# A spectral mixing kernel: the last transform stage runs two units behind the mixing, and the shrinking becomes one ScalarE Relu and one VectorE pass

## The chip, the cores and the metric

The kernel runs on one core of a Trainium2 chip. Its time is the device time of one execution in microseconds (us). TensorE (PE) multiplies matrices, VectorE (DVE), ScalarE (ACT) and GpSimd (POOL) work elementwise, and SyncE (SP) only issues transfers. Each engine works through its own queue in order and waits on semaphores for the others. Matmul results land in PSUM, which has eight banks; everything else sits in SBUF or in device memory.

## What is computed

For each of 8 batches of 3072 x 256 values, the reference takes a real Fourier transform along the sequence, mixes the 256 channels with a complex matrix, adds a bias, shrinks both parts towards zero by 0.01 and transforms back. A feed-forward network with two weight matrices and a piecewise square gate follows.

```python
X = np.fft.rfft(x, axis=1)
Yr = Xr @ w_r - Xi @ w_i + b_r
Yi = Xr @ w_i + Xi @ w_r + b_i
Yr = np.sign(Yr) * np.maximum(np.abs(Yr) - lam, 0.0)
Yi = np.sign(Yi) * np.maximum(np.abs(Yi) - lam, 0.0)
y = np.fft.irfft(Yr + 1j * Yi, n=3072, axis=1)
h = y @ w_in
g = np.where(h >= 1, h, np.where(h <= -1, 0.0, (h + 1) ** 2 / 4))
out = g @ w_out
```

## The kernel before

The transform is cut into factors of 48 and 64. Stage 1 is the 48-point factor over half batches of rows, stage 2 the 64-point factor, then the channels are mixed, then stages 3 and 4 undo the two factors. Products are made with operands split into a rounded part (hi) and a rest (lo), three matmuls to a product.

**The mixing loop** (`for u in range(UN + 3)`, `UN` = 96) handles one unit per iteration: two of the 24 frequency groups of a batch, so 12 units (`NU`) to a batch. The order in which instructions are recorded is the order in which each engine's queue holds them; nothing rearranges them. In iteration u the kernel records:

- `split_X_hi` (L258): two ScalarE copies of stage 2's result of unit u-1 out of PSUM, `Xd` (the imaginary half) and `Xh` (the rounded whole);
- `difference` (L267): VectorE makes the difference `Xd` of the two halves. For the first unit of a batch it also makes a few two-column tiles (`Xe`, `e0`);
- `mix_shared` (L307): six matmuls of unit u-2 into the bank `ps_mix`; `take_shared` (L313): VectorE adds the bias to the result and keeps it as `shift`;
- `split_X_lo` (L283) and `split_difference` (L288): the rests `Xl`, `Xdl` on VectorE and the rounded `Xdh` on ScalarE;
- `stage3` (L342) of unit u-3: matmuls that read `y` of that unit, and a ScalarE copy `ust` of the result, which `store_u` writes to `u_d` one iteration later;
- `stage1` in the iterations that have one (two of three after the first batch, none in the last ones), with two ScalarE copies;
- `mix_rest` (L319): twelve matmuls of unit u-2 on top of the same bank, six more for a batch's first unit; `add_bias` (L327): VectorE adds `shift` and writes `y`;
- `shrink` (L332): VectorE clamps `y` to +-0.01 (`yc`, L335) and subtracts that from `y` (L336);
- `stage2` (L241) of unit u.

So `stage3` of unit u-3 in iteration u needs the `shrink` that was recorded at the end of iteration u-1. Between the two, TensorE has `stage2` of unit u-1 and `mix_shared` of unit u-2.

Three calls `weights()` in an iteration convert the network's double precision weights a step at a time, two units to a weight (32 weights, so some 64 units from u = 2 on); the steps run on VectorE (`man`, `scl`), ScalarE (`parts`, `winh`, `wout`) and GpSimd (`both`, `wpair`, `winl`). `half4` runs stage 4 on an eighth of the first batch; eight of them are spread over the last iterations. The network follows the loop and runs on from there.

`ust` and `ps_mix` have two buffers, `y` (tag `ya`) two, `yc` (tag `yb`) one, and stage 3's bank (tag `E`) one.

Of the kernel before, what the change touches and what calls it, by code (L numbers as in the profile page):

```python
# [10 lines left out]
F32 = mybir.dt.float32  # L11
# [5 lines left out]
P = 128  # L17
# [86 lines left out]
def tile_fft_mix_moe(  # L104
# [44 lines left out]
    z_first = keep.tile([P, G, D], F32, tag="wout", name="z_first")  # L149
    c2_sb = keep.tile([P, R1], F32, name="c2_sb")  # L150
    half = keep.tile([P, 1], F32, name="half")

    c1_sb = first_st.tile([P, 2, HP], F32, name="c1_sb")
    t_sb = mixing.tile([P, G, P], F32, name="t_sb")
# [76 lines left out]
                nc.sync.dma_start(zh[b][k, :, j : j + HT, :], z[e * HP : e * HP + R1])  # L231


    zin, xp, dp, yp, ust = {}, {}, {}, {}, {}

    def load_z(u):
        b, v = divmod(u, NU)
# [20 lines left out]
    def split_X_hi(u):  # L258
        ps = xp[u]
        _, im = both(ps)  # L260
        dp[u] = mixing.tile([P, ND, P], F32, tag="Xd", name="Xd")
        nc.scalar.copy(dp[u], im)
        hi = mixing.tile([P, ND, 2, 2, R2], F32R, tag="Xh", bufs=2, name="Xh")
        nc.scalar.copy(hi, ps)
        xp[u] = ps, hi

    def difference(u):  # L267
        ps, _ = xp[u]
        re, _ = both(ps)
        dif = dp[u]  # L270
        at = slice(0, 1)
        if u % NU == 0:
            e = mixing.tile([P, ND, 1], F32, tag="Xe", name="Xe")
            nc.vector.scalar_tensor_tensor(
                out=e, in0=re[:, :, at], scalar=-1.0, in1=dif[:, :, at], op0=ALU.mult, op1=ALU.subtract
            )
            split(nc.vector, e0[0][:, :, at], e0[1][:, :, at], e)
        nc.vector.tensor_tensor(out=dif, in0=re, in1=dif, op=ALU.subtract)
        if u % NU == 0:
            nc.vector.tensor_copy(dif[:, :, at], re[:, :, at])  # L280

    def split_X_lo(u):
        ps, hi = xp[u]  # L283
        lo = mixing.tile([P, ND, 2, 2, R2], F32R, tag="Xl", bufs=2, name="Xl")
        nc.vector.tensor_tensor(out=lo, in0=ps, in1=hi.bitcast(F32), op=ALU.subtract)
        xp[u] = hi, lo

    def split_difference(u):  # L288
        dif = dp[u]
        hi, lo = dp[u] = [mixing.tile([P, ND, P], F32R, tag=f"Xd{k}", bufs=2, name=f"Xd{k}") for k in "hl"]  # L290
        nc.scalar.copy(hi, dif)
        nc.vector.tensor_tensor(out=lo, in0=dif, in1=hi.bitcast(F32), op=ALU.subtract)

    def mixed(out, pairs, start):
        n = 0
# [13 lines left out]
    def mix_shared(u):  # L309
        ps = yp[u] = pools["ps"].tile([P, 2, D], F32, tag="C", bufs=2, name="ps_mix")  # L310
        mixed(ps[:, 0, :], [(dp.pop(u), "i")], True)
# [15 lines left out]
    def add_bias(u):  # L327
        y = fold.tile([P, 2, D], F32, tag="ya", bufs=2, name="y")
        nc.vector.tensor_tensor(out=y, in0=yp[u], in1=shift, op=ALU.add)  # L329
        yp[u] = y  # L330

    def shrink(u):  # L332
        y = yp[u]
        c = fold.tile([P, 2, D], F32, tag="yb", name="yc")
        nc.vector.tensor_scalar(out=c, in0=y, scalar1=-LAM, scalar2=LAM, op0=ALU.max, op1=ALU.min)  # L335
        nc.vector.tensor_tensor(out=y, in0=y, in1=c, op=ALU.subtract)  # L336

    def stage3(u):
        b, v = divmod(u, NU)
        y = yp.pop(u)  # L340
        ps = pools["ps"].tile([P, 2, 2, D], F32, tag="E", name="ps_i1")[:, :, 0, :]
        for c in range(2):  # L342
            for gi in range(2):
                rows = slice(gi * HP, (gi + 1) * HP)
                nc.tensor.matmul(  # L345
                    ps[:, gi, :],
                    lhsT=ti_sb[rows, v, c, :],
                    rhs=y[rows, c, :],
                    start=c == 0,
                    stop=c == 1,  # L350
                    tile_position=(gi * HP, 0),
                )
        ust[u] = fold.tile([P, 2, D], F32, tag="ust", bufs=2, name="ust")
        nc.scalar.copy(ust[u], ps)

    def store_u(u):
        b, v = divmod(u, NU)
        nc.sync.dma_start(ug[b][:, 2 * v : 2 * v + 2, :], ust.pop(u))
# [292 lines left out]
    with tc.manual_schedule():  # L651
# [3 lines left out]
        idle = win[0][NP - 1][:, 0:1, :]  # L655
        nc.vector.memset(idle.bitcast(F32), 0.0)
        nc.vector.memset(half, 0.5)
        for x in e0:
            nc.vector.memset(x.bitcast(F32), 0.0)
        wst = []  # L660
# [53 lines left out]
        def half4(tags="AB"):  # L714
            c = next(four)
            stage4(c, [bank(k, 2 if k == "D" else 1) for k in tags])
            stage4_out(c, [nc.scalar.copy] * 2)

        U4 = UN - 8

        U_IN = UN - NU + 2

        WU = 2
        for u in range(UN + 3):
            hs_u = halves(u)
            at = lambda lag: 0 <= u - lag < UN
            weights = more_weights if WU <= u < 85 else lambda: None
            while stored < hs_u.start:
                store_z(stored)
                stored += 1  # L730
            if at(4):
                store_u(u - 4)
            if u == NU:
                wout = keep.tile([P, NF, 2, D], F32R, tag="wout", name="wout")
            if u + 1 < NU:
                load_ti(u + 1)
            if 0 < u < NU - 2:
                load_t(2 * u + 4, 2 * u + 6)
            if u == WU - 1:
                load_weights(0)  # L740
                load_weights(1)
            if u == 10:
                nc.sync.dma_start(c2_sb, c2)
            if NU <= u + 2 < UN:
                load_z(u + 2)
            if at(1):
                split_X_hi(u - 1)
                difference(u - 1)
            if at(2):
                mix_shared(u - 2)  # L750
                take_shared(u - 2)
            if at(1):
                split_X_lo(u - 1)
                split_difference(u - 1)
            weights()
            if at(3):
                stage3(u - 3)
            for h in hs_u:
                stage1(h, "AB", [nc.scalar.copy] * 2)
                x_ahead(h)  # L760
            if U4 <= u < U4 + 4 or u == UN:
                half4()
            weights()
            if at(2):
                mix_rest(u - 2)
                add_bias(u - 2)
                weights()
                shrink(u - 2)
            if u < UN:
                stage2(u)  # L770
            if u == U_IN:
                for _ in ws:
                    pass
                first_st.release()
                pools["in"] = right("in")
                pools["ops0"] = right("ops0")
                for c in range(3):
                    load_u(c)
            if u == UN - 3:
                prep_sums(0)  # L780
            if u == UN - 2:
                prep_split_hi(0, 0)
                prep_split_lo(0, 0)
            if u == UN - 1:
                prep_split_hi(0, 1)
                prep_split_lo(0, 1)
            if u == UN + 1:
                half4("DD")
                half4("AB")
                prep_split_hi(0, 2)  # L790
                prep_split_lo(0, 2)
                half4("DD")
        store_u(UN - 1)
        mixing.release()
        pools["ops1"] = right("ops1")
# [111 lines left out]
```

## Time and profile before

| | us |
|---|---|
| median of 3 runs | 2720.39 (2718.38 to 2722.28) |
| the profiled execution, its own time | 2722.25 |
| span of its trace, first to last instruction | 2720.3 |
| PE busy | 2636.1 (97%) |
| DVE busy | 2055.2 (76%) |
| ACT busy | 1622.5 (60%) |
| POOL busy | 330.7 (12%) |
| stage 3's first and last matmul start | 42.6 and 594.9 |

The trace gives the span; the execution's own time is 2 us more, for what lies around it. The last row bounds the mixing loop; the rest of the span is the network.

### The profile page before, as it was taken

The page shows a single profiled execution, that of the slowest core. Times are in us where ns is not written, and L with a number is a line of the kernel's source. Part 1 is how long each engine was busy: PE and PEld are TensorE (multiplying, and loading weights), DVE is VectorE, ACT ScalarE, POOL GpSimd, SP SyncE. Part 2 cuts the span into 40 slices and gives each one's busy share as a digit, 9 for nine tenths or more (in the row PEclk, how much of TensorE's full clock was granted, in tenths as well). Part 3 has the DMA queues.
Part 4 walks back from the last instruction along what each step waited for, and adds up shares of the span by engine and source line. Part 5 has one row for each costly group of instructions (what it writes and reads, how often), then busy time and mean ns, then how long its engine had stood idle before and what let it go on. Part 6 is the DMA issues. An engine that isn't in the chain of part 4 may idle for free.

```text
span 2720.3 us, 54586 instructions
## 1 busy us (share of the span) xinstructions
PE 2636.1 (97%) x22600; PEld 2385.1 (88%) x22600; DVE 2055.2 (76%) x3075; ACT 1622.5 (60%) x2909; POOL 330.7 (12%) x325
## 2 busy tenths in 40 slices
PE   8888889989999999999999999999999999999998
PEld 6666777779999999999999999999999999999998
DVE  5778886668777777777777777777777777777776
ACT  4445554446666666666666666666666666666665
POOL 2333220001000101001010101010101101010100
PEclk8999999999999999999999999999999999999999
DMA  7666766530000000000101000000000000100000
GB/s 218 193 191 198 208 203 187 146 101 9 22 25 23 26 22 27 23 26 22 31 22 30 21 28 21 28 20 28 21 28 21 28 27 22 34 15 23 9 17 16
DMA packets 114951, 160.65 MB, mean 59 GB/s; under 512 B 13072, under 2 KB 87440, under 8 KB 114704
## 3 DMA queue, kind: packets, MB, share of 16 engines
q1 hardware_dynamic: 114424, 156.97, 19.9%
q8 instruction: 178, 2.92, 0.4%
q14 instruction: 69, 0.57, 0.1%
q10 hardware_dynamic: 280, 0.20, 0.0%
HBM read 84.76 MB, written 72.35 MB: 58 GB/s over the span
## 4 chain that ended last, share of the span: by engine, by line
PE 90%; DVE 7%; ACT 1%; issue 1%; DMA 0%; SPq 0%; ACTq 0%
PE ps_xv L548 20%; PE ps_yz L548 15%; PE accB L604 13%; PE accA L604 13%; PE accB L607 7%; PE accA L607 7%; PE ps_mix L299 5%; PE ps_i L345 3%; PE ps_i L472 3%; PE ps_f L213 2%; DVE y L336 2%; DVE y L329 2%; DVE yc L335 1%; PE ps_f L247 1%; DVE scl L398 1%
## 5 line engine op out<-in xcount | busy, mean ns | idle before, releaser
L556 ACT COPY snap<-ps_xv 128x256 f32<-128x256 f32 x1152 | 424.2, 368 | 764.1 <-PE ps_xv L548 764.1
L590 DVE TENSOR_TENSOR gl<-h,gh 128x1024 fp32r<-128x1024 f32 x385 | 470.6, 1222 | 270.3 <-ACT gh L586 270.3
L560 DVE CUSTOM_DVE_ANT_0 h<-ps_yz,snap 128x256 f32<-128x256 f32 (+1 forms) x768 | 428.2, 558 | 227.6 <-PE ps_yz L548 194.6
L604 PE MATMUL accA<-wout,gh 128*128 128x512 f32 x1536 | 570.7, 393 | 0.0
L604 PE MATMUL accB<-wout,gh 128*128 128x512 f32 x1536 | 562.0, 399 | 0.0
L581 DVE SCALAR_TENSOR_TENSOR h<-h,r 128x1024 f32<-128x1024 f32 x385 | 480.7, 1249 | 0.0
L577 ACT ACTIVATE r<-h,half 128x1024 f32<-128x1024 f32 x385 | 443.3, 1151 | 2.0 <-DMA u_d<-ust 2.0
L548 PE MATMUL ps_xv<-oph,winh 128*128 128x256 f32 x1536 | 436.5, 284 | 1.2 <-ACT snap L556 0.9
L548 PE MATMUL ps_xv<-opl,winh 128*128 128x256 f32 x1536 | 433.5, 282 | 0.0
L607 PE MATMUL accB<-wout,gl 128*128 128x256 f32 x1536 | 432.4, 282 | 0.0
L607 PE MATMUL accA<-wout,gl 128*128 128x256 f32 x1536 | 431.4, 281 | 0.8 <-DVE gl L590 0.7
L548 PE MATMUL ps_xv<-oph,winl 128*128 128x256 f32 x1536 | 430.0, 280 | 0.0
L586 ACT CAST gh<-h 128x1024 fp32r<-128x1024 f32 x385 | 404.4, 1050 | 4.2 <-DVE h L581 4.1
L503 POOL TENSOR_TENSOR tsum<-yt 128x256 f32<-128x256 f32 x96 | 106.7, 1131 | 1982.1 <-DVE opl L524 1103.0
L604 PEld LDWEIGHTS accB<-wout,gh 128*128 128x128 f32 x1536 | 289.7, 189 | 56.8
L548 PE MATMUL ps_yz<-oph,winl 128*128 128x256 f32 x1152 | 326.2, 283 | 0.0
L548 PE MATMUL ps_yz<-oph,winh 128*128 128x256 f32 x1152 | 323.5, 281 | 1.9 <-DVE h L560 1.8
L548 PE MATMUL ps_yz<-opl,winh 128*128 128x256 f32 x1152 | 324.5, 282 | 0.0
L604 PEld LDWEIGHTS accA<-wout,gh 128*128 128x128 f32 x1536 | 287.8, 187 | 35.2
L548 PEld LDWEIGHTS ps_xv<-oph,winh 128*128 128x128 f32 x1536 | 288.0, 188 | 32.4 <-ACT snap L556 2.0
L548 PEld LDWEIGHTS ps_xv<-oph,winl 128*128 128x128 f32 x1536 | 291.2, 190 | 0.0
L607 PEld LDWEIGHTS accA<-wout,gl 128*128 128x128 f32 x1536 | 288.8, 188 | 1.8 <-DVE gl L590 1.8
(106 smaller groups left out, 4282.3 us busy)
## 6 DMA issues: line engine op xcount, KB each, us to landing
u_d<-ust SPq DMA_DIRECT2D x96, 256.0 KB
uin<-u_d SPq DMA_DIRECT2D x128, 192.0 KB
out<-ot SPq DMA_DIRECT2D x191, 128.0 KB
xin<-in_x SPq DMA_DIRECT2D x112, 192.0 KB
z_d<-zst SPq DMA_DIRECT2D x224, 96.0 KB
zin<-z_d SPq DMA_DIRECT2D x84, 256.0 KB
wraw<-in_moe_w_in SPq DMA_DIRECT2D x16, 256.0 KB
wraw<-in_moe_w_out SPq DMA_DIRECT2D x16, 256.0 KB
```

The costliest lines, as they stand in the source:

```text
L299: nc.tensor.matmul(out, lhsT=a[:, d], rhs=wm[nm, k][:, d, :], start=start and n == 0, stop=n == 3 * ND * len(pairs) - 1, skip_group_check= ...
L345: nc.tensor.matmul(ps[:, gi, :], lhsT=ti_sb[rows, v, c, :], rhs=y[rows, c, :], start=c == 0, stop=c == 1, tile_position=(gi * HP, 0),)
L503: nc.gpsimd.tensor_tensor(out=t[:, to], in0=a, in1=b, op=ALU.subtract)
L548: nc.tensor.matmul(ps, lhsT=win[a][p][:, w, :], rhs=mv[:, m, :], start=start and k == 0, stop=k == 2, skip_group_check=True)
L556: nc.scalar.copy(snaps[n][:, at, :], ups[n][1][:, 0, :])
L560: nc.vector._custom_dve(TENSOR_ADD_SAT, out=out, in0=a, in1=b, s0=FLT_MAX, s1=-1.0)
L577: nc.scalar.activation(rs[n][:, part], hs[n][:, part], AF.Square, bias=half, scale=0.5)
L581: nc.vector.scalar_tensor_tensor(out=h, in0=h, scalar=1.0, in1=r, op0=ALU.max, op1=ALU.min)
L586: nc.scalar.copy(gs[n][0][:, part], hs[n][:, part])
L590: nc.vector.tensor_tensor(out=gl, in0=hs[n][:, part], in1=gh.bitcast(F32), op=ALU.subtract)
L604: nc.tensor.matmul(o, lhsT=gh[:, blk, at : at + P], rhs=wout[:, f], start=f == 0, stop=False, skip_group_check=True)
L607: nc.tensor.matmul(o[:, 0, :], lhsT=gl[:, blk, at : at + P], rhs=wout[:, f, 0, :], start=False, stop=f == NF - 1, skip_group_check=True,)
```

## The change

`shrink` becomes two operations. `above` is a ScalarE activation, `over` = Relu(y - 0.01), with the constant -0.01 in a new one-column tile `lam`. `shrink` is one VectorE pass, min(y + 0.01, over). Both now belong to the iteration after `add_bias`, and `stage3` comes one iteration later again: unit u-4 instead of u-3. `store_u` moves along, and the loop has one more iteration. On VectorE the pass stands behind `Xdl`; on ScalarE `above` stands behind `Xdh`, which is now recorded ahead of `Xl`. The stage 4 calls near the end are spread differently.

```diff
     def split_difference(u):
         dif = dp[u]
...
         nc.scalar.copy(hi, dif)
-        nc.vector.tensor_tensor(out=lo, in0=dif, in1=hi.bitcast(F32), op=ALU.subtract)
+        return lambda: nc.vector.tensor_tensor(out=lo, in0=dif, in1=hi.bitcast(F32), op=ALU.subtract)
...
+    def above(u):
+        over[u] = fold.tile([P, 2, D], F32, tag="yb", name="over")
+        nc.scalar.activation(over[u], yp[u], AF.Relu, bias=lam)
+
     def shrink(u):
         y = yp[u]
-        c = fold.tile([P, 2, D], F32, tag="yb", name="yc")
-        nc.vector.tensor_scalar(out=c, in0=y, scalar1=-LAM, scalar2=LAM, op0=ALU.max, op1=ALU.min)
-        nc.vector.tensor_tensor(out=y, in0=y, in1=c, op=ALU.subtract)
+        nc.vector.scalar_tensor_tensor(out=y, in0=y, scalar=LAM, in1=over.pop(u), op0=ALU.add, op1=ALU.min)
...
-        U4 = UN - 8
+        U4 = (UN - 9, UN - 8, UN - 6, UN - 5)
...
-        for u in range(UN + 3):
+        for u in range(UN + 4):
...
-            if at(4):
-                store_u(u - 4)
+            if at(5):
+                store_u(u - 5)
...
             if at(1):
                 split_X_hi(u - 1)
+            if at(2):
+                mix_shared(u - 2)
+            if at(1):
                 difference(u - 1)
             if at(2):
-                mix_shared(u - 2)
                 take_shared(u - 2)
             if at(1):
+                rest = split_difference(u - 1)
+            if at(3):
+                above(u - 3)
+            if at(1):
                 split_X_lo(u - 1)
-                split_difference(u - 1)
+                rest()
+            if at(3):
+                shrink(u - 3)
             weights()
-            if at(3):
-                stage3(u - 3)
+            if at(4):
+                stage3(u - 4)
...
-            if U4 <= u < U4 + 4 or u == UN:
+            if u in U4 or u == UN:
                 half4()
             weights()
+            if u == UN + 1:
+                half4("DD")
             if at(2):
                 mix_rest(u - 2)
                 add_bias(u - 2)
                 weights()
-                shrink(u - 2)
...
-            if u == UN - 2:
-                prep_split_hi(0, 0)
-                prep_split_lo(0, 0)
-            if u == UN - 1:
-                prep_split_hi(0, 1)
-                prep_split_lo(0, 1)
-            if u == UN + 1:
+            if UN - 2 <= u < UN + 1:
+                prep_split_hi(0, u - UN + 2)
+                prep_split_lo(0, u - UN + 2)
+            if u == UN + 2:
                 half4("DD")
-                half4("AB")
-                prep_split_hi(0, 2)
-                prep_split_lo(0, 2)
-                half4("DD")
+            if u == UN + 3:
+                half4()
```

VectorE's queue before, in a unit without weight steps, from one `add_bias` to the next (a name's number is its buffer; `ps_f2` is stage 2's bank):

```order
L329 TENSOR_TENSOR y_5986<-ps_mix_5943,shift_117 128x512
L335 TENSOR_SCALAR yc_5988<-y_5986 128x512
L336 TENSOR_TENSOR y_5986<-y_5986,yc_5988 128x512
L278 TENSOR_TENSOR Xd_6003<-ps_f2_5991,Xd_6003 128x256
L315 TENSOR_TENSOR shift_117<-ps_mix_6008,bias_i_118 128x256
L285 TENSOR_TENSOR Xl_6016<-ps_f2_5991,Xh_6005 128x512
L292 TENSOR_TENSOR Xdl_6019<-Xd_6003,Xdh_6018 128x256
L329 TENSOR_TENSOR y_6041<-ps_mix_6008,shift_117 128x512
```

The two passes that finish `y_5986` stand right behind the one that writes it. The same stretch of VectorE's queue with the change:

```order
L330 TENSOR_TENSOR y_6483<-ps_mix_6439,shift_118 128x512
L279 TENSOR_TENSOR Xd_6509<-ps_f2_6485,Xd_6509 128x256
L316 TENSOR_TENSOR shift_118<-ps_mix_6513,bias_i_119 128x256
L286 TENSOR_TENSOR Xl_6527<-ps_f2_6485,Xh_6511 128x512
L293 TENSOR_TENSOR Xdl_6523<-Xd_6509,Xdh_6522 128x256
L339 SCALAR_TENSOR_TENSOR y_6483<-y_6483,over_6525 128x512
L330 TENSOR_TENSOR y_6590<-ps_mix_6513,shift_118 128x512
```

`Xd`, `shift`, `Xl` and `Xdl` now stand between the pass that writes `y_6483` and the one that finishes it, and one pass is gone. ScalarE's queue with the change, over a unit with a stage 1:

```order
L263 COPY Xd<-ps_f_5534 128x256
L265 CAST Xh<-ps_f_5534 128x512
L292 CAST Xdh<-Xd 128x256
L335 ACTIVATE over<-y,lam 128x512
L357 COPY ust<-ps_i_5568 128x512
L224 COPY zst<-ps_f_5575 128x512
L224 COPY zst<-ps_f_5576 128x512
```

The Relu is new, between `Xdh` and `ust`; the others stood in this order before.

## Rows read from the trace of the kernel before

**Rows 1.** Windows by stage: mixing loop with weights, network. Busy us of each engine, clock, DMA

```profile
core 0: us, PE busy (x) PEld busy (x) DVE busy (x) ACT busy (x) POOL busy (x), PEclk, DMA share, GB/s
43.00:425.00 382.00, 332.26 (x2558) 262.45 (x2554) 304.62 (x629) 196.31 (x430) 115.24 (x120) 0.98 0.68 200
...
595.00:2720.00 2125.00, 2114.70 (x17796) 1966.27 (x17792) 1620.01 (x2160) 1333.55 (x2274) 204.32 (x188) 1.00 0.08 24
```

**Rows 2.** Lines, 0 to 620 us: busy, mean ns, idle before, releasers

```profile
L345 PE MATMUL ps_i<-y,ti_sb 64*128 64x256 f32 x768 | 109.2, 399 | 66.5 <-DVE y L336 54.9 <-ACT Xh L264 5.5 <-DVE Xe L274 3.1
...
L329 DVE TENSOR_TENSOR y<-ps_mix,shift 128x512 f32<-128x512 f32 x96 | 66.2, 690 | 131.1 <-PE ps_mix L299 131.1
...
L354 ACT COPY ust<-ps_i 128x512 f32<-128x512 f32 x96 | 56.2, 586 | 40.8 <-PE ps_i L345 29.3 <-DMA u_d<-ust 7.0 <-issue 3.9
...
L335 DVE TENSOR_SCALAR yc<-y 128x512 f32<-128x512 f32 x96 | 52.5, 547 | 2.2
...
L437 POOL TENSOR_TENSOR winl<-wpair,winh 128x896 fp32r<-128x896 f32 x8 | 16.9, 2113 | 49.0 <-ACT winh L436 49.0
```

**Rows 3.** Timeline of a unit without stage 1: start, us, engine, instruction, wait

```profile
570.56 1.05 PE L247 MATMUL ps_f<-t_sb,zin 128*128 128x128 f32 x8
...
571.92 0.59 ACT L264 CAST Xh<-ps_f 128x512 fp32r<-128x512 f32 x1
571.95 0.69 DVE L336 TENSOR_TENSOR y<-y,yc 128x512 f32<-128x512 f32 x1
572.05 0.28 PE L299 MATMUL ps_mix<-wm_ih,Xdl 128*128 128x256 f32 x1
572.56 0.42 DVE L278 TENSOR_TENSOR Xd<-ps_f,Xd 128x256 f32<-128x256 f32 x1
572.79 1.13 PE L345 MATMUL ps_i<-y,ti_sb 64*128 64x256 f32 x8 [0.46 <-DVE y L336]
572.89 0.41 DVE L315 TENSOR_TENSOR shift<-ps_mix,bias_i 128x256 f32<-128x256 f32 x1
...
573.85 0.39 PE L299 MATMUL ps_mix<-wm_bh,Xh 128*128 128x256 f32 x1
...
575.38 0.39 PE L247 MATMUL ps_f<-t_sb,zin 128*128 128x128 f32 x2
```

**Rows 4.** Timeline, PE in a unit with a stage 1

```profile
465.55 1.09 PE L213 MATMUL ps_f<-xin,c_sb 48*64 48x512 f32 x8
...
466.57 0.39 PE L299 MATMUL ps_mix<-wm_bh,Xh 128*128 128x256 f32 x1
```

**Rows 5.** Timeline, PE at 130 us: stage 3 right behind the shared product

```profile
129.85 0.28 PE L299 MATMUL ps_mix<-wm_ih,Xdl 128*128 128x256 f32 x1
130.06 1.13 PE L345 MATMUL ps_i<-y,ti_sb 64*128 64x256 f32 x8
```

**Rows 6.** Timeline at 116 to 122 us, and windows after two such places

```profile
116.48 2.25 DVE L398 SCALAR_TENSOR_TENSOR scl<-wraw,scl 128x256 uint32<-128x256 uint32 x1
...
121.63 1.33 PE L345 MATMUL ps_i<-y,ti_sb 64*128 64x256 f32 x8 [2.48 <-DVE y L336]
...
125.00:150.00 25.00, 22.10 (x160) 17.79 (x160) 19.15 (x38) 12.65 (x27) 8.32 (x9) 0.91 0.67 198
200.00:225.00 25.00, 22.13 (x160) 17.78 (x160) 19.12 (x38) 12.59 (x27) 8.34 (x9) 0.91 0.67 197
```

**Rows 7.** The page's groups: two ScalarE operations of the network, 1024 wide

```profile
L577 ACT ACTIVATE r<-h,half 128x1024 f32<-128x1024 f32 x385 | 443.3, 1151 | 2.0 <-DMA u_d<-ust 2.0
...
L586 ACT CAST gh<-h 128x1024 fp32r<-128x1024 f32 x385 | 404.4, 1050 | 4.2 <-DVE h L581 4.1
```

**Rows 8.** Timeline: a store of `ust` on SP's queue, and its buffer's next copy

```profile
431.18 0.43 SPq L358 DMA_DIRECT2D u_d<-ust  x1
...
438.50 0.59 ACT L354 COPY ust<-ps_i 128x512 f32<-128x512 f32 x1 [0.54 <-DMA u_d<-ust]
```

**Rows 9.** Timeline, DVE in the first unit: from `Xe` to `Xl`

```profile
31.39 0.16 DVE L274 SCALAR_TENSOR_TENSOR Xe<-ps_f,Xd 128x2 f32<-128x2 f32 x1 [0.19 <-ACT Xh L264]
...
32.40 0.68 DVE L285 TENSOR_TENSOR Xl<-ps_f,Xh 128x512 fp32r<-128x512 f32 x1
```

More of the change, by code (lines that the diff above doesn't have):

```diff
@@ L151, in tile_fft_mix_moe @@
     half = keep.tile([P, 1], F32, name="half")
+    lam = keep.tile([P, 1], F32, name="lam")
     c1_sb = first_st.tile([P, 2, HP], F32, name="c1_sb")
@@ L231, in store_z @@
                 nc.sync.dma_start(zh[b][k, :, j : j + HT, :], z[e * HP : e * HP + R1])
-    zin, xp, dp, yp, ust = {}, {}, {}, {}, {}
+    zin, xp, dp, yp, over, ust = {}, {}, {}, {}, {}, {}
     def load_z(u):
@@ L657, in tile_fft_mix_moe @@
         nc.vector.memset(half, 0.5)
+        nc.vector.memset(lam, -LAM)
         for x in e0:
```

## The prediction, made before the changed kernel had run

> **What bounds the kernel now.** I read the windows by stage first. In the network TensorE is busy 2114.70 of 2125.00 us, and nothing there changes. In the mixing loop with weights it is busy 332.26 of 382.00 us while VectorE is at 304.62, 80% [rows 1]: neither is full, so they wait for each other. The table of lines says where. Stage 3's matmuls (L345) find TensorE idle for 66.5 us in all, 54.9 of it ended by the subtracting pass of the shrinking; VectorE in turn is idle 131.1 us before `add_bias`, always for `ps_mix` [rows 2]. That is a ring: mixing, `add_bias`, two passes, stage 3, mixing again.
>
> One unit of the timeline shows the ring [rows 3]. The last shared product starts at 572.05, the subtraction runs from 571.95 to 572.64, and stage 3 starts at 572.79 after 0.46 us of idle TensorE. From stage 2 to the next stage 2 it takes 575.38 - 570.56 = 4.82 us. A stage 1 adds 466.57 - 465.55 = 1.02 us [rows 4], so 5.84.
>
> **What goes.** Stage 3 of a unit is now recorded a whole iteration after the `shrink` that it needs, so its wait should vanish. Three terms:
>
> 1. The idle time itself: 66.5 us [rows 2].
> 2. A little more than the idle time, because a waiting TensorE also drains. With the wait, stage 3 starts 572.79 - 572.05 = 0.74 us after the last product [rows 3]; where nothing had to be waited for, 130.06 - 129.85 = 0.21 us [rows 5]. The saving is 0.53 a unit where the idle time is 0.46, so 0.06 more for each of 95 gaps: 5.7 us.
> 3. The slow clock. At 121.63 stage 3 had waited 2.48 us. The window that follows shows a mean granted clock of 0.91, and so does the one at 200 us [rows 6]. The granted clock has two levels, 1.2 and 2.4 GHz, so these are stretches at the lower one. The unit from 121.63 [rows 6] to 130.06 [rows 5] takes 8.43 us, where a unit with a stage 1 takes 5.84. Twice 2.6 is 5.2 us, and it goes if no wait of that size is left.
>
> Together 77.4 us. TensorE executes the same instructions as before, so this is also what is left above its own work: 1.49 (570.56 to 572.05) + 0.21 + 1.06 (stage 3 to mixing) + 1.53 (mixing to stage 2) = 4.29 us a unit [rows 3, 5], against 4.82.
>
> **What the change adds, and what hides it.**
>
> - *The Relu*, 96 times on ScalarE. No row shows it. Its floor is a plain copy of the same width, 0.586 (`ust`) [rows 2]; its ceiling an activation with a bias column at twice the width, 1.15 [rows 7]. I take the copy and what such a bias activation costs over a cast of equal width, 1.15 - 1.05: 0.69 us. ScalarE is busy 196.31 of 382 us [rows 1]; with 64 x 0.69 = 44 us more it is at 240 of about 326, so it stays hidden. Behind the Relu wait `ust` and stage 1's copies, and `ust` is not due until stage 3 has ended.
> - *The single pass* takes the place of two. It reads two SBUF inputs of the same width as the subtraction, so 0.69 [rows 3]; from below it is bounded by the clamp, 0.547 on average [rows 2], from above by a pass that is held up (below, 1.84 more). What goes from VectorE is the clamp.
> - *The next ring.* What is late next? `mix_rest` may not overwrite the bank before `shift` has been taken from it, `shift` stands behind `Xd`, and `Xd` waits for `Xh`. From stage 2's start: `Xh` ends at 572.51, 1.95 later; `Xd` starts 0.05 after that, `shift` 0.33 later and lasts 0.41: 2.74 [rows 3]. TensorE reaches `mix_rest` at 1.49 + 0.21 + 1.06 = 2.76. This is a dead heat in a unit without a stage 1, and 1.02 us of room in one that has it. So nothing is lost in an ordinary unit, but in a unit without stage 1 whatever delays VectorE is paid at once.
> - *A batch's first unit.* From `Xe` to `Xl` VectorE needs 1.01 us [rows 9], where `Xd` alone takes 0.33 [rows 3]: 0.68 more ahead of `shift`. One iteration later there is a second `shift` pass, 0.41. Eight batches make 8.7 us; a third of them without a stage 1 to hide it: 2.9 us.
> - *The long GpSimd operation.* Eight times `winl` runs for 2.11 us [rows 2], and a VectorE pass of 256 columns then takes 2.25 [rows 6] instead of the 0.41 that `shift`, as wide, needs [rows 3]: 1.84 late. VectorE's slack a unit is 131.1/96 = 1.37, plus the clamp 0.55, minus the shortening 77.4/95 = 0.81: 1.1. So 0.74 of it comes through where no stage 1 hides it, a third of eight: 2.0 us.
> - *The tail.* The last unit's `y`, Relu and pass take 3 x 0.69 = 2.1 us; TensorE has stage 3 of the unit before (1.06) and an eighth of stage 4 of about a stage 1's length (1.02) to do meanwhile. The extra iteration adds no matmul. I count the moved pieces of stage 4, their loads and the moved `store_u` (one queue, same order on SP) at nothing; what covers them is matmul work of the same iteration. If that cover were gone it would cost one wait of `Xh`'s chain each, 0 to 2 us in all.
>
> Sum: 77.4 - 2.9 - 2.0 = 72.5 us. The profiled execution took 2722.25, its span 2720.3; 2722.25 - 72.5 = 2649.8. The median of the runs lies 1.9 below the profiled one, so I predict **2648**.
>
> **Rivals.**
>
> *A. GpSimd takes back half of the gain in the weights stage.* The passes `Xdl` and `shrink` both read two SBUF inputs. GpSimd is busy 115.24 of 382 us in 120 operations [rows 1], 30% of the time, 0.96 us each. A pass that begins at random finds one running 0.30 of the time and waits half of it, 0.48: for two passes 0.29 us a unit, 18.5 us over 64 units, and the eight `winl` at their full 1.84 give 14.7. If no slack takes any of that, 77.4 - 2.9 - 33.2 = 41 are left: 2679. For it: rows 6 shows the hold-up. Against: VectorE's slack of 1.1, and that `Xd`, `shift`, `Xl` and `y` read PSUM. The Trainium skill, page "SBUF — State Buffer", section "SBUF: two separate sides", states that a VectorE operation with two SBUF inputs and a GpSimd operation that reads SBUF exclude each other for a whole instruction, and the loser blocks fully. By that rule the new pass is held up just as the old ones were, and the time tends to this rival's. The trace agrees in the one place quoted, 2.25 us beside a 2.11 us operation.
>
> *B. The stores set the pace.* `ust` has two buffers. A store issued at 431.18 has its buffer overwritten at 438.50, 7.3 us later, and the profile names that store as the last thing waited for, though the 0.54 us there is no more than the ordinary wait [rows 8]. Two units that are each 0.53 shorter leave 6.3. If landing takes 7.3, ScalarE waits 1.06 every two units and the floor of 0.46 a unit is not gained: 66.5 - 95 x 0.46 + 5.2 = 28 us, 2692. Against: the DMA share is 0.68 [rows 1], so the transfers are not full.
>
> *C. Slower.* In the weights units without a stage 1, a third of 64 or some 21, a hold-up of VectorE goes straight to `mix_rest`. If in each of them a GpSimd operation made it 2.5 us late, TensorE would fall to its lower clock as after the 2.48 us wait [rows 6], and lose 2.5 + 2.6 = 5.1 each: 107 us in 21, 2648 + 107 = 2755. It turns to slower from 16 such units on (16 x 5.1 = 82 against 72.5 + 5.4). Against: only `winl` is that long, and there are eight [rows 2].
>
> *D. The wait only changes its place.* If VectorE ran a whole unit behind TensorE, stage 3 would wait for the later pass as it did for the earlier one, and the time would stay at 2720. Against: VectorE is the one that waits, 131.1 us [rows 2].
>
> **How the numbers follow.** The forecast has a chance of 0.70, A 0.15, B 0.06, C 0.04, D 0.05. The forecast's own bounds: with none of the added costs 2722.25 - 77.4 - 1.9 = 2643, less 2 for the spread of the runs, 2641; upwards it passes into A, and 2684 holds A with a little over. Below 2641 and above 2684 lie B, C, D and the edges, 2 in 10. What a measurement can tell from no change is about 0.2%, 5.4 us: faster by more is the forecast, A and B, 0.91; the same is D, 0.05; slower is C, 0.04.
>
> **What would show it.** Right: L345's idle time falls from 66.5 to under 10; units without a stage 1 take 4.3 us and those with it 5.3; the clock in the 125 and 200 us windows is 1.0; a Relu row of 0.65 to 0.75 us, 96 times; `mix_rest` after a batch's first unit shows a short wait for `shift`. Wrong: idle time before `mix_rest` in most weights units (A, or C if the clock falls too), `ust` starting later after stage 3 than before with its store named (B), stage 3 still waiting (D).

## The result, and the profile after

The changed kernel takes **2636.36 us** (median of 4 runs, 2635.85 to 2639.13); the kernel before took 2721.34 in the same comparison (4 runs). The ratio is 0.9691, with a 95% interval of 0.9674 to 0.9708. The prediction was 2648 with a range from 2641 to 2684: the direction came out, and in the mixing loop the mechanism too; the time lies 4.6 us below the range. The profiled execution took 2636.4 us, its span is 2634.6.

The page after, busy time and chain. TensorE now makes nearly the whole chain.

```profile
PE 2617.0 (99%) x22600; PEld 2371.2 (90%) x22600; DVE 1998.6 (76%) x2980; ACT 1670.1 (63%) x3005; POOL 331.5 (13%) x325
...
PE 98%; DVE 1%; ACT 1%; issue 0%; DMA 0%; ACTq 0%
```

Windows after, columns as in [rows 1]: the loop with weights, and the two windows that had shown the slow clock.

```profile
43.00:425.00 382.00, 381.63 (x3021) 299.66 (x3019) 300.07 (x641) 262.40 (x568) 115.49 (x120) 1.00 0.78 230
...
125.00:150.00 25.00, 24.95 (x200) 19.86 (x199) 21.77 (x45) 17.69 (x39) 10.93 (x12) 1.00 0.83 248
200.00:225.00 25.00, 24.96 (x199) 19.82 (x199) 20.93 (x47) 17.99 (x39) 6.70 (x6) 1.00 0.84 246
```

TensorE is busy 381.63 of 382 us where it had been 332.26 [rows 1], and both later windows show a granted clock of 1.00 instead of 0.91 [rows 6]. ScalarE rose to 262.40 us, VectorE stays at 300.

The table of lines after, whole span: busy, mean ns, idle before and releasers.

```profile
L348 PE MATMUL ps_i<-y,ti_sb 64*128 64x256 f32 x768 | 108.9, 402 | 0.3 <-DVE y L339 0.3
L335 ACT ACTIVATE over<-y,lam 128x512 f32<-128x512 f32 x96 | 69.0, 719 | 2.3 <-DVE y L330 2.3
L339 DVE SCALAR_TENSOR_TENSOR y<-y,over 128x512 f32<-128x512 f32 x96 | 67.4, 702 | 0.8 <-ACT over L335 0.8
...
L330 DVE TENSOR_TENSOR y<-ps_mix,shift 128x512 f32<-128x512 f32 x96 | 65.8, 686 | 41.1 <-PE ps_mix L300 41.1
L300 PE MATMUL ps_mix<-wm_bh,Xh 128*128 128x256 f32 x192 | 64.5, 336 | 1.5 <-DVE shift L316 0.6 <-DVE shift L318 0.4
L357 ACT COPY ust<-ps_i 128x512 f32<-128x512 f32 x96 | 54.5, 568 | 0.6 <-PE ps_i L348 0.6
```

Stage 3's wait of 66.5 us [rows 2] is 0.3. The new wait is the one before `mix_rest` (L300, `wm_bh`), 1.5 us in all. `ust` waits 0.6 us, for no store.

A unit without a stage 1 after, timeline of PE, DVE and ACT, for [rows 3].

```profile
436.39 1.05 PE L248 MATMUL ps_f<-t_sb,zin 128*128 128x128 f32 x8
...
437.75 0.59 ACT L265 CAST Xh<-ps_f 128x512 fp32r<-128x512 f32 x1
...
437.87 0.27 PE L300 MATMUL ps_mix<-wm_ih,Xdl 128*128 128x256 f32 x1
438.07 1.13 PE L348 MATMUL ps_i<-y,ti_sb 64*128 64x256 f32 x8
438.37 0.42 DVE L279 TENSOR_TENSOR Xd<-ps_f,Xd 128x256 f32<-128x256 f32 x1 [1.09 <-ACT Xh L265]
438.71 0.41 DVE L316 TENSOR_TENSOR shift<-ps_mix,bias_i 128x256 f32<-128x256 f32 x1
...
439.18 0.39 PE L300 MATMUL ps_mix<-wm_bh,Xh 128*128 128x256 f32 x1
439.97 0.68 DVE L339 SCALAR_TENSOR_TENSOR y<-y,over 128x512 f32<-128x512 f32 x1
440.70 0.50 PE L248 MATMUL ps_f<-t_sb,zin 128*128 128x128 f32 x3
```

Stage 3 starts 0.20 us behind the last shared product, as in [rows 5]. `shift` ends at 439.12 and `mix_rest` starts at 439.18: the dead heat. From one unit's stage 2 to the next it is 4.31 us; over the trace such units take 4.31 to 4.42 us, and nearly all with a stage 1 take 5.30 to 5.36 (a batch's first unit, with six matmuls more, 5.99).

**Where the 85.7 us of span came from.** The network can be cut out exactly by its first and last gate operation on VectorE. Before, then after:

```profile
605.01 1.22 DVE L581 SCALAR_TENSOR_TENSOR h<-h,r 128x1024 f32<-128x1024 f32 x1
...
2709.45 0.69 DVE L581 SCALAR_TENSOR_TENSOR h<-h,r 128x512 f32<-128x512 f32 x1
```

```profile
526.20 1.21 DVE L584 SCALAR_TENSOR_TENSOR h<-h,r 128x1024 f32<-128x1024 f32 x1
...
2623.79 0.69 DVE L584 SCALAR_TENSOR_TENSOR h<-h,r 128x512 f32<-128x512 f32 x1
```

| stretch | before | after | gain |
|---|---|---|---|
| span's start to the third unit's first shared product | 41.25 | 38.86 | 2.4 |
| from there to the first gate (the loop) | 563.76 | 487.34 | 76.4 |
| first gate to last gate (the network) | 2104.44 | 2097.59 | 6.85 |
| last gate to the end | 10.85 | 10.81 | 0.0 |

The first row is scatter: two other profiles of the same two kernels (e1, e2) have 39.46 and 39.85 there. The loop comes near the forecast: 76.4 us here and 74.2 between e1 and e2, where 72.5 had been forecast. The network, in which the change edits no instruction, is 6.85 us faster.

### The profile page after: what moved, and what is told of

Its sections match the earlier page's. It is cut to its first block, busy times and chain, and to the rows that moved or that the text cites. A ratio compares the mean times of both kernels' runs of the same rounds, so it can differ in the third digit from the quotient of the medians.

```text
span 2634.6 us, 54676 instructions
## 1 busy us (share of the span) xinstructions
PE 2617.0 (99%) x22600; PEld 2371.2 (90%) x22600; DVE 1998.6 (76%) x2980; ACT 1670.1 (63%) x3005; POOL 331.5 (13%) x325
## 4 chain that ended last, share of the span: by engine, by line
PE 98%; DVE 1%; ACT 1%; issue 0%; DMA 0%; ACTq 0%
PE ps_xv L551 21%; PE ps_yz L551 16%; PE accB L607 14%; PE accA L607 13%; PE ps_mix L300 9%; PE accA L610 7%; PE accB L610 7%; PE ps_i L348 4%; PE ps_f L248 3%; PE ps_i L475 3%; PE ps_f L214 2%; PE ps_f L192 0%; PE warm L673 0%; DMA u_d<-ust 0%; ACT gh L589 0%
```

## The experiments

All runs are on one core. e1, e5 and e12 to e16 are single executions, the others medians of 4 to 10. A ratio is always to the kernel before, timed beside that run. "Network" is the time from the first gate to the last, "loop" that from the third unit's first shared product to the first gate.

**e1 and e2: both kernels again.** No edit. Is the network's gain there again?

> The kernel before, unchanged, for its profile on this chip. In the profiles at hand the network's units take 5.472 us before and 5.454 with the change, 0.33% less though no line of the network differs, 6.9 us in all. Theory P (the place of things in SBUF: the new column lies in front of the network's tiles): 5.472 here. Theory R (the rate belongs to the chip or the occasion): the same figure as every other kernel of this call, whichever that is.

> The changed kernel, unchanged. Both theories: 0.969 of the kernel before. P: units of the network of 5.454. R: the figure of the first kernel of this call.

e1: 2717.29 us, network 2104.45, loop 560.6. e2: 2637.55 us (ratio 0.9705, 0.9691 to 0.9719), network 2097.63, loop 486.4. The network's 6.8 us come back to within 0.05: they belong to the kernel, not to the occasion.

**e3 and e4: the change's one-column tile alone, and the change with that tile elsewhere.**

e3, against the kernel before:

```diff
+    lam = keep.tile([P, 1], F32, name="lam")
...
+        nc.vector.memset(lam, -LAM)
```

e4, against the changed kernel:

```diff
-    lam = keep.tile([P, 1], F32, name="lam")
...
+    lam = fold.tile([P, 1], F32, name="lam")
```

> The kernel before with nothing but the one-column tile added and filled. P: network units of 5.454, 7 us faster than before (0.9975). R: network units as in the kernel before on this chip, 1.000.

> The changed kernel with the column in the pool that is given back ahead of the network, so that the network's tiles lie as before. P: network units of 5.472, 7 us slower than the changed kernel, 0.9715 of before. R: as the changed kernel, 0.969.

e3: 2711.74 us, ratio 0.9979 (0.9970 to 0.9989); network 2097.63. e4: 2643.72 us, ratio 0.9727 (0.9713 to 0.9742); network 2104.43. The first and last gate of e3:

```profile
602.38 1.22 DVE L582 SCALAR_TENSOR_TENSOR h<-h,r 128x1024 f32<-128x1024 f32 x1
...
2700.01 0.69 DVE L582 SCALAR_TENSOR_TENSOR h<-h,r 128x512 f32<-128x512 f32 x1
```

So the network's gain has nothing to do with lags or Relu. `lam` holds one number per partition, occupies 32 bytes in the built program, and pushes every tile allocated behind it on that side of SBUF up by 32 bytes (`gh`, the rounded part of the gate's result, from byte 118112 to 118144). In e4 `gh` is back at 118112, and the gain is gone.

**e7 and e8: lag and Relu apart.** e7 keeps the later stage 3 and the moved shrinking, with the two old passes in place of Relu and one pass. e8 is the kernel before with `lam`, and with Relu and pass in the old place.

e7, against the changed kernel (`shrink` is clamp and subtraction again):

```diff
-            if at(3):
-                above(u - 3)
```

e8, against e3 (`above` and `shrink` as in the change):

```diff
                 weights()
+                above(u - 2)
                 shrink(u - 2)
```

> The changed kernel with the shrinking left as the two VectorE passes of before (clamp, subtract), placed where the change has its one pass, no Relu; the later stage 3 and all else of the change stay. Theory L, the one unit more before stage 3 gives nearly all of the gain and the Relu only relieves VectorE: in the change VectorE is busy 41 to 43 us of each 50 us up to 350 us, 0.7 us more a unit brings that to some 48 or 49, so a few more waits there and none behind; the first gate at 530 to 540 us instead of 526.2, 2640 to 2651 us in all. Rival R, the shorter chain through the Relu is what saves: less than half of the gain of the loop remains, first gate later than 560 us, over 2672 us in all. The network takes 2097.6 us by either.

> The kernel before with the tile of one column and the shrinking as a Relu on ScalarE and one VectorE pass, but in its old place, right behind the addition of the bias, stage 3 as early as before. Theory L: the chain from the addition to stage 3 gets longer, since Relu and pass (0.72 and 0.70 us and two changes of engine) take the place of clamp and subtraction (0.55 and 0.69): 0.2 to 0.4 us a unit if all of it is waited for, at most 20 to 40 us; the VectorE relief gives some of it back: 2705 to 2750 us in all, not faster than the 2711.7 us of the kernel before with the column by more than 7. Rival R, that VectorE is relieved by 0.55 us a unit is what counts: 2690 us or less. The network takes 2097.6 us by either.

e7: 2641.66 us, ratio 0.9717 (0.9703 to 0.9732), first gate 531.18. e8: 2724.17 us, ratio 1.0018 (1.0009 to 1.0028), first gate 617.81. That is 12.4 us above e3, or 10.8 if the 1.7 us are taken off by which the kernel before was slower beside it. Both runs come out as theory L has it; the rivals are out. Lines of e8, 43 to 640 us:

```profile
L348 PE MATMUL ps_i<-y,ti_sb 64*128 64x256 f32 x766 | 109.5, 405 | 81.4 <-DVE y L339 81.4
L339 DVE SCALAR_TENSOR_TENSOR y<-y,over 128x512 f32<-128x512 f32 x95 | 70.4, 741 | 74.9 <-ACT over L335 74.9
```

Without the lag the Relu lengthens the ring: stage 3 waits 81.4 us instead of 66.5 [rows 2], and VectorE stands idle 74.9 us for ScalarE. In e7 a `winl` on GpSimd shows what the two passes cost where VectorE is full. Its POOL, DVE and PE rows at 145 to 150 us:

```profile
144.98 2.21 POOL L442 TENSOR_TENSOR winl<-wpair,winh 128x896 fp32r<-128x896 f32 x1 [3.20 <-ACT winh L441]
...
145.25 2.48 DVE L341 TENSOR_TENSOR y<-y,yc 128x512 f32<-128x512 f32 x1
...
149.72 0.39 PE L300 MATMUL ps_mix<-wm_bh,Xh 128*128 128x256 f32 x1 [0.44 <-DVE shift L316]
```

The subtraction takes 2.48 us beside it, VectorE has no gap in the operations behind it up to `shift`, and TensorE waits 0.44.

**e11 and e18: stage 3 alone later.** Both keep stage 3 two units behind the mixing, and put the shrinking back right behind the sum: e11 as Relu and pass, e18 as the two old passes. Against the changed kernel (e18 has no `above`, and its `shrink` is clamp and subtraction):

```diff
-            if at(3):
-                above(u - 3)
-            if at(3):
-                shrink(u - 3)
...
                 add_bias(u - 2)
                 weights()
+                above(u - 2)
+                shrink(u - 2)
```

> The changed kernel with Relu and pass right behind the addition of the bias, where before had its two passes, instead of one unit later; stage 3 stays two units behind the mixing. Theory L, stage 3's lag alone takes its wait away, but the shrinking's place counts for VectorE: it would wait there for the Relu, and the next unit's difference (0.6 us after its own input is there) would come 0.3 to 0.6 us later in the units without stage 1, and the mixing with it: 10 to 25 us of the gain lost, first gate at 536 to 552 us, 2646 to 2662 us in all. Rival O, the order on VectorE is indifferent once stage 3 has its slack: 2634 to 2640 us, first gate at 526 to 529 us.

> The changed kernel with the shrinking as the two VectorE passes of before and in their old place, right behind the addition, so that stage 3 alone comes a unit later. Theory W, what e11 lost was VectorE's wait for the Relu (0.85 us in a unit): without it the next difference starts as soon as its input is there, as it did in the kernel before, and the time is near that of e7 with its two passes one unit later, first gate at 530 to 542 us, 2640 to 2652 us in all. Rival O2, the place ahead of the next unit's difference costs by itself, since nothing may go before the passes on VectorE: as much as in e11 or more, first gate at 555 us or later, 2665 us or more. The network takes 2097.6 us by either.

e11: 2673.7 us, ratio 0.9833 (0.9820 to 0.9847), first gate 563.47. e18: 2656.75 us, ratio 0.9778 (0.9762 to 0.9795), first gate 546.25. e11 lost 36 to 37 us where 10 to 25 had been expected; e18 lies between its two theories, nearer to W. Lines of e11, then of e18, 43 to 640 us:

```profile
L348 PE MATMUL ps_i<-y,ti_sb 64*128 64x256 f32 x768 | 108.9, 402 | 0.3 <-DVE y L339 0.3
L339 DVE SCALAR_TENSOR_TENSOR y<-y,over 128x512 f32<-128x512 f32 x95 | 72.4, 762 | 74.5 <-ACT over L335 74.5
...
L300 PE MATMUL ps_mix<-wm_bh,Xh 128*128 128x256 f32 x189 | 63.5, 336 | 34.5 <-DVE shift L316 30.9 <-DVE shift L318 2.8
```

```profile
L350 PE MATMUL ps_i<-y,ti_sb 64*128 64x256 f32 x768 | 108.9, 402 | 0.0
...
L300 PE MATMUL ps_mix<-wm_bh,Xh 128*128 128x256 f32 x190 | 63.5, 334 | 19.6 <-DVE shift L316 16.9 <-DVE shift L318 2.1
```

In both, stage 3 no longer waits, and the wait turns up before `mix_rest`: what stands ahead of the next `Xd` on VectorE delays `shift`. What delays it differs. DVE in a unit without a stage 1, e11:

```profile
452.31 0.69 DVE L330 TENSOR_TENSOR y<-ps_mix,shift 128x512 f32<-128x512 f32 x1 [0.85 <-PE ps_mix L300]
453.85 0.69 DVE L339 SCALAR_TENSOR_TENSOR y<-y,over 128x512 f32<-128x512 f32 x1 [0.85 <-ACT over L335]
454.60 0.42 DVE L279 TENSOR_TENSOR Xd<-ps_f,Xd 128x256 f32<-128x256 f32 x1
454.94 0.41 DVE L316 TENSOR_TENSOR shift<-ps_mix,bias_i 128x256 f32<-128x256 f32 x1
```

`y` starts at 452.31 and `Xd` 2.29 us later, since VectorE waits 0.85 for the Relu in between; after the change that distance is 438.37 - 436.59 = 1.78. The unit takes 4.82 us again.

In e18 such a unit loses nothing: below, from 455.92, `Xd` starts 1.80 us after `y`, and the next `y` follows 4.33 us after the first. The loss comes earlier. Of the 19.6 us before `mix_rest`, 16.7 lie before 380.5 us, while the weights are being converted. POOL, DVE and PE rows of e18, first in a unit of that stage, then the DVE rows of one behind it:

```profile
249.84 1.28 POOL L408 TENSOR_TENSOR both<-parts,scl 128x512 f32<-128x512 f32 x1 [0.42 <-DVE scl L403]
250.48 0.93 DVE L340 TENSOR_SCALAR yc<-y 128x512 f32<-128x512 f32 x1
...
252.86 0.39 PE L300 MATMUL ps_mix<-wm_bh,Xh 128*128 128x256 f32 x1 [0.48 <-DVE shift L316]
...
455.92 0.69 DVE L330 TENSOR_TENSOR y<-ps_mix,shift 128x512 f32<-128x512 f32 x1 [0.85 <-PE ps_mix L300]
456.65 0.43 DVE L340 TENSOR_SCALAR yc<-y 128x512 f32<-128x512 f32 x1
...
457.72 0.41 DVE L279 TENSOR_TENSOR Xd<-ps_f,Xd 128x256 f32<-128x256 f32 x1
...
460.25 0.69 DVE L330 TENSOR_TENSOR y<-ps_mix,shift 128x512 f32<-128x512 f32 x1 [0.85 <-PE ps_mix L300]
```

Beside a GpSimd operation (`both`) the clamp takes 0.93 us instead of 0.43, and with the passes ahead of `Xd` that delay goes on to `shift` and TensorE.

The loop's times then split the change into its steps. With `lam` in place throughout (e3, e18, e7, after): 562.9, 505.4, 492.5, 487.3. So, in this order, **57.5 us come from stage 3's lag, 12.9 from moving the shrinking behind the next unit's VectorE work, and 5.2 from Relu and one pass**, which alone (e8) cost some 11 to 12. With Relu and pass already in, the same move of the shrinking is worth 36 (e11). The 57.5 also hold the moved pieces of stage 4, which no run takes apart, and two falls of the clock, which e3 has and e18 has not. Two profiles of one kernel differ by 1 us (after) to 3 us (before) in this stretch.

**e5, e6, e9, e10, e12 to e16: where the tiles lie.** First theory: an operand should start on a multiple of 64 bytes. `gh` starts 32 over one in the kernel before and on one after; `oph`, the products' moving operand, starts 32 over one in both. e5 widens `lam` in e3 to 64 bytes; the others move the right side of SBUF, where `oph` and `opl` lie, by a pad of 1 column (32 bytes: e6 and e9 on the change, e12 on the kernel before) or of 16, 24 or 32 columns (64, 96 or 128 bytes: e13, e15 and e17; e10 and e16; e14):

```diff
+    pad = right("pad")
+    gap = pad.tile([P, 1], F32, name="gap")
     first_st = right("first")
```

e9 and e10 widen a small tile besides:

```diff
-            e = mixing.tile([P, ND, 1], F32, tag="Xe", name="Xe")
+            e = mixing.tile([P, ND, 8], F32, tag="Xe", name="Xe")[:, :, 0:1]
```

> The kernel before plus a tile of 16 columns (64 bytes) where the change has its tile of one column (which takes 32 bytes). Theory A, the network is faster when the tiles gh and gl, the stationary operands of the down-projection, start on a multiple of 64 bytes: they are back on 32 over a multiple of 64, so from the network's first gate to its last it takes the 2104.4 us of the kernel before (5.472 us a unit), about 2718 us in all. Rival B, any shift of those tiles away from where they were helps (a distance between two tiles, not an alignment): the network stays at 2097.6 us (5.454), about 2711 us in all.

> The changed kernel with everything on the right side of the memory moved down by 32 bytes (one more tile of one column, allocated first there), so that the network's moving operands oph and opl, which start 32 over a multiple of 64 bytes, start on a multiple of 64 as gh and gl do. Theory A1, the place matters for every operand of a matmul: the network's 16 products a unit gain 1 to 2 ns each as well, 6 to 12 us over 385 units, so 2086 to 2092 us from first to last gate and 2625 to 2631 us in all. Rival A2, only the stationary operand's place matters (the product's stationary tiles win start on a multiple of 64 already): 2097.6 us for the network and 2636 to 2638 us in all. Rival A3, products lose by it: slower than 2640 us.

> The kernel of e6 (changed kernel, right side moved by 32 bytes) with the small tile Xe widened from 2 to 16 numbers (64 bytes instead of 32), so that the loop's Xdh, Xdl, Xl and zin, stationary operands of the mixing and of stage 2, start on a multiple of 64 bytes too. Theory A1, the place matters for every operand: about 18 matmuls of a unit gain 1 to 1.5 ns each, 2 to 3 us over the loop's 96 units, so the first gate at 522 to 523.5 us instead of 525.15, 2626 to 2627.5 us in all. Rival A4, the loop shows nothing of it since other waits fill in: first gate at 525 to 526, 2628 to 2630 us. The network stays at 2089.6 us.

> The kernel of e9 with the right side moved by 96 bytes instead of 32, so that oph and opl start on a multiple of 128 bytes, as gh, gl, win and wout do; in e6 and e9 they start 64 over one. Theory A64, what counts is a multiple of 64: the network takes 2089.6 us as in e6, the total that of e9. Rival A128, a multiple of 128 is better still: the network gains as much again, 2080 to 2086 us, and the total is 4 to 10 us below that of e9.

> The kernel before, with only its right side moved by 32 bytes: gh and gl stay 32 over a multiple of 64, oph and opl come onto one. Theory A1, each operand's place counts by itself: the network gains the 8 us that it gained in e6, 2095.5 to 2097.5 us instead of 2104.4, and 2709 to 2712 us in all. Rival A5, both operands must lie on a multiple before anything is gained there: 2103 to 2104.5 us, 2716 to 2720 us in all.

e5: 2719.72 us, network 2103.06. e6: 2629.2 us (ratio 0.9670, 0.9656 to 0.9685), network 2089.61. Both are near what the alignment theory has, though e5 lies 1.3 us off the 2104.4 that it should have come back to. Then the theory fell. e12, with `gh` off the multiple, has 2084.14 (2694.05 us in all), less than e6 and outside both expectations. e10, with every operand of the network's matmuls on a multiple of 128, has 2109.49 (2648.07 us, 0.9735, 0.9720 to 0.9750), the slowest network of all. e9: 2626.49 us (0.9658, 0.9645 to 0.9671), network 2089.58; its loop is 486.1 us against 486.4 in e6, so the loop's operands show nothing of it (the 2.7 us between the medians come in part from the start: third shared product at 37.59 instead of 38.78).

Two further theories (e13, e14 and e16 on e4's kernel, e15 on the change), on the distance between the sides (D) and on places that repeat after 128 bytes (M):

> The changed kernel with the tile of one column in the pool fold (as e4: the left side of the network lies as in the kernel before, shift 0) and the right side moved by 64 bytes. The network's times so far, by left shift and right shift in bytes: 0,0 2104.4; 32,0 2097.6; 64,0 2103.1; 32,32 2089.6; 32,96 2109.5; 0,32 2084.1. Theory D, the network's time is one term for the left shift (the down-projection) and one for the sum of both shifts (the distance of oph from the left side's tiles): 13.5 us less than the same sum at left shift 32, so 2103.1 and 2089.6 give 2076.1 us, 2616 us in all. Theory M, the product's time depends on where oph lies by itself within 128 bytes: 32 over a multiple there, a place not yet tried; between 2084 and 2110 us.

> As e13 with the right side moved by 128 bytes. Theory D: the sum of the shifts is that of e10 (128), less 13.5 us: 2096 us for the network, 2635 us in all. Theory M, places repeat after 128 bytes: the time of right shift 0, 2104.4 us for the network, 2643 to 2644 us in all. Neither: outside both.

> The changed kernel (left shift 32) with the right side moved by 64 bytes. Theory D: the sum 96 has not been tried, but the time is 13.5 us above that of e16. Theory M: oph lies 32 over a multiple of 128 as in e13, and the network's time differs from e13's by what the left shift gave at right shift 0 or 32, -7 to +6 us.

> As e13 with the right side moved by 96 bytes. Theory D: 13.5 us below e15. Theory M: oph starts on a multiple of 128 as in e10, and the network is within -6 to +7 us of e10's 2109.5 us.

The network's time, first gate to last gate, by the shift in bytes of the left side (up, against the kernel before) and of the right side (down):

| left \ right | 0 | 32 | 64 | 96 | 128 |
|---|---|---|---|---|---|
| 0 | 2104.4 (before, e1, e4) | 2084.1 (e12) | 2079.9 (e13, e17) | 2096.5 (e16) | 2089.6 (e14) |
| 32 | 2097.6 (after, e2, e3, e7, e8, e11, e18) | 2089.6 (e6, e9) | 2084.2 (e15) | 2109.5 (e10) | |
| 64 | 2103.1 (e5) | | | | |

e13 gives 2079.9 where D had 2076.1 and M 2084 or more; e14 gives 2089.6 where D had 2096 and M 2104.4; e15 is 12.3 us below e16 where D had it 13.5 above; e16 is 13 us below e10 where M had at most 6. Both theories fall, and the rule stays open. The table is reproducible: the seven profiles with left shift 32 and right shift 0 (also e11 and e18), whatever their loop, lie between 2097.58 and 2097.64 us. The time goes in the matmuls. The products' rows of e6 and of e10, whole span:

```profile
L553 PE MATMUL ps_xv<-oph,winh 128*128 128x256 f32 x1536 | 430.7, 280 | 1.4 <-ACT snap L561 1.3
L553 PE MATMUL ps_xv<-opl,winh 128*128 128x256 f32 x1536 | 429.2, 279 | 0.0
```

```profile
L553 PE MATMUL ps_xv<-oph,winh 128*128 128x256 f32 x1536 | 435.2, 283 | 1.4 <-ACT snap L561 1.3
L553 PE MATMUL ps_xv<-opl,winh 128*128 128x256 f32 x1536 | 434.4, 283 | 0.0
```

The instruction and the idle time are the same, and each is recorded as 3 to 4 ns longer. The records overlap, so this is not yet what the network loses. Adding up the time from each matmul's start to the next one's start, from the traces, gives it (us; 8015 matmuls of the products, 6124 of the down-projection, which multiplies `gh` and `gl` by `wout`):

| | left, right | products | down-projection |
|---|---|---|---|
| before | 0, 0 | 965.8 | 1078.2 |
| after | 32, 0 | 966.1 | 1071.0 |
| e12 | 0, 32 | 942.2 | 1081.4 |
| e13 | 0, 64 | 947.5 | 1071.9 |
| e6 | 32, 32 | 951.2 | 1078.0 |
| e10 | 32, 96 | 963.0 | 1086.0 |

From e6 to e10 a product matmul loses 1.5 ns. `lam` gives its gain in the down-projection alone, 7.2 us, where `gh` and `gl` had moved. But in e13 the down-projection gains 6.3 us against the kernel before, although `gh`, `gl` and `wout` lie where they lay before: only the tiles of the right side had moved. So the addresses of a matmul's own operands are not the whole cause.

**e17: the best of them.** e13's kernel (the change, `lam` in `fold`, right side 64 bytes lower), in four executions.

> The kernel of e13 again, timed in rounds: whether its one look holds. The network takes 2079.9 us and all of it 2617 to 2622 us, 14 to 19 us below the changed kernel, if the place of the tiles alone sets it; if the single look was a lucky occasion, 2625 us or more.

2620.02 us (4 runs, 2617.67 to 2620.85), ratio 0.9643 (0.9629 to 0.9658), network 2079.86. It beats both kernels, the changed one by some 16 us. Its first and last gate:

```profile
527.86 1.22 DVE L586 SCALAR_TENSOR_TENSOR h<-h,r 128x1024 f32<-128x1024 f32 x1
...
2607.72 0.69 DVE L586 SCALAR_TENSOR_TENSOR h<-h,r 128x512 f32<-128x512 f32 x1
```

## Why the prediction was wrong, point by point

**The step that failed is in the first paragraph: "nothing there changes", said of the network.** Of the 85.7 us of span, 6.85 were gained there. The diff had the cause in plain sight, one more tile in the pool that lies ahead of the network's tiles, but the working priced `lam` at nothing without a word on it. With that term 2648 would have been 2641.2, and the lower end of the range 2634, below the 2636.4 measured. The runs e3 and e4 show the step: `lam` alone takes the network from 2104.4 to 2097.6 us.

**Second, the added costs of 4.9 us were too high.** All waits of TensorE left in the loop add up to 1.8 us (0.3 before stage 3, 1.5 before `mix_rest`); 77.4 - 1.8 = 75.6, against 76.4 and 74.2 measured. By terms:

- *Idle time 66.5, drain 5.7, slow clock 5.2*: right for the profile that they were read from (0.53 - 0.46 is 0.07 and not 0.06, 1 us in all). Stage 3's wait is 0.3, units without a stage 1 take 4.31 to 4.42 where 4.29 was forecast, and no window from 45 to 517 us shows a granted clock below 1.00. The slow clock is not the same in every execution of the kernel before. In windows of 25 us it falls at two places in the profile of [rows 6], in e3 and in e5 (0.86 at 120 to 145 and at 195 to 220 us), at one place in e1 (0.96 and 0.90 at 170 to 220 us), and nowhere in e12 (the kernel before with its right side moved). The loops take 563.8, 562.9 and 563.6, then 560.6, then 558.2 us: 2.4 to 3.2 us for a fall, where 2.6 was forecast.
- *Relu and pass*: 0.72 and 0.70 us, forecast 0.69 each. Both hidden.
- *The next ring*: the dead heat was there, at 0.02 to 0.13 us a unit. What the prediction didn't say is how much hangs on what stands ahead of `Xd`: the two passes there cost 12.9 us (e18), most of it while GpSimd works on the weights, and Relu and pass cost 36 (e11), in plain units too.
- *A batch's first unit*: forecast 2.9 for a third of eight batches, measured 1.06, at two places of the last batch (timeline of PE after):

```profile
452.80 0.38 PE L300 MATMUL ps_mix<-wm_bh,Xh 128*128 128x256 f32 x1 [0.64 <-DVE shift L316]
...
457.57 0.39 PE L300 MATMUL ps_mix<-wm_bh,Xh 128*128 128x256 f32 x1 [0.42 <-DVE shift L318]
```

  A batch has 12 units and stage 1 comes in two of three, so every batch's first unit stands in the same phase, and that phase has a stage 1. Only the last batch, behind the last stage 1, pays. A share (a third) was taken where the pattern could have been counted.
- *The long GpSimd operation*: forecast 2.0. The hold-up happens and costs almost nothing. POOL and DVE after:

```profile
204.16 2.11 POOL L440 TENSOR_TENSOR winl<-wpair,winh 128x896 fp32r<-128x896 f32 x1 [4.40 <-ACT winh L439]
...
204.28 2.26 DVE L401 SCALAR_TENSOR_TENSOR scl<-wraw,scl 128x256 uint32<-128x256 uint32 x1
206.47 0.68 DVE L330 TENSOR_TENSOR y<-ps_mix,shift 128x512 f32<-128x512 f32 x1
```

  `scl` is the operation hit, 2.25 to 2.27 us beside each of the eight `winl`, and VectorE's slack takes it up: TensorE waits before `mix_rest` behind two of them only, 0.02 us each. Eleven more waits of 0.01 to 0.07 us before `mix_rest` at this stage, some 0.3 us in all, come behind no `winl`.

**The rivals.** *A*: the Trainium skill's page "SBUF — State Buffer", section "SBUF: two separate sides", has the loser block for a whole instruction, and 2.26 us beside 2.11 agrees; but what it would take back was not taken back. The hold-up stopped being harmless in e7, where VectorE had 0.7 us more a unit to do (2641.66 us instead of 2636 to 2638), and in e18, where the passes stood ahead of `Xd`. *B*: `ust` waits 0.6 us and for stage 3. *C*: no such waits. *D* is what e11 shows in part: stage 3 free, and half of the wait moved to `mix_rest`.

**The range.** Its lower end of 2641 was the sum without any added cost, less 2 us for scatter. It held no term for a stage left alone, and so the measured 2636.4 fell outside.

## What to carry to other kernels

Giving a consumer one more unit of lag removes its wait only if nothing then stands in the way of the next one: find what the late engine has queued ahead of the work that the bottleneck needs next, and move that too (here 57.5 us for the lag, 12.9 for the place of the passes, 5.2 for shortening them, and a loss where the shortening came alone). Count a pattern that repeats instead of taking a share of it. Before crediting an edit with a small gain, look at a stage that it doesn't touch: a tile added anywhere moves others, and a pad of a few bytes is a variant to be timed like any other.

## What was not expected of the hardware

The start address of SBUF tiles changes the rate of otherwise equal matmuls. Over ten placements that differ by multiples of 32 bytes, the same network took between 2079.9 and 2109.5 us, 1.4% of it; placements with equal offsets agreed within 0.06 us in kernels whose loops differed. Alignment to 64 or to 128 bytes, the distance between the two sides, and a repeat after 128 bytes were each tried and each failed. Since the down-projection changed by 6.3 us in e13 with its own operands in place, the addresses of a matmul's own operands can't be all of it. Whether the rest is a meeting with what VectorE and ScalarE read and write at the same time was not tried and is open; a pad moves every tile of its side at once (left `snap`, `h`, `r`, `gh`, `gl`; right `oph`, `opl`, `uin`, `yt`, `tsum`), so the table doesn't tell which tile does it.
